# A blockwise causal attention feeding a gated FFN: zeros as weights of the warming matmuls, and three more head pairs transposed by DMA

## The chip, the cores and the metric

The kernel runs on one core of a Trainium2 chip. The metric is the device time of one execution in microseconds (us); lower is better. A core has a tensor engine (PE, with a separate row PEld for its weight loads), a vector engine (DVE), a scalar engine (ACT), a general engine (POOL) and a sync engine (SP) that here only issues DMAs. In the profile a name with a "q" (SPq, ACTq, POOLq) is the engine's instruction sequencer, which among other things issues DMAs; "L707" is line 707 of the kernel.

## The reference

Eight batches, eight heads, 576 tokens, head size 64. Attention is causal by blocks of 64 tokens; its output, with the heads side by side, is the input of a feed-forward layer with a ReLU gate.

```python
scores = scale * q @ k^T                      # per batch and head, 576 x 576
scores = where(block_i >= block_j, scores, -1e9)
attn = softmax(scores)
x = (attn @ v)  ->  [8 * 576, 512]            # tokens x (8 heads x 64)
out = (relu(x @ w_gate) * (x @ w_val)) @ w_out   # 512 -> 1536 -> 512
```

## The kernel before

The schedule is written out by hand: every engine executes its instructions in the order in which the program names them. The unit of the attention is a round `r` = 4 x batch + head pair, 32 rounds in all. Rounds 0 to 7 are written out one by one; rounds 8 to 31 are the loop at line 1008. Between the pieces of a round stand pieces of the FFN: `ffn(n)` takes the next matmuls from a generator that walks through the batches one after the other, so that PE always has work.

One round of the loop does, in this order on each engine:

1. `head_av(r - 1, 0)` (L648, PE): attention times values of the previous round's first head, with the exponentials in `attnT` as weights.
2. `scores_all(r)` (L514, PE): three pieces of scores into three pairs of PSUM banks, and four exponentials by ACT (L520) into one of two buffers `attnT`.
3. `head_av(r - 1, 1)`, then `heads_to_xnat(r - 1)`: a reciprocal and a product on DVE (L592, L593) write the normalised output, tokens on partitions, into the tile `xnat`. There are three `xnat` buffers, so round r + 3 writes the buffer of round r.
4. A transpose that puts features on partitions, as the FFN needs them: 512 tokens go into `xT` (three buffers, one per batch), the last 64 tokens of the batch into `xTt`. There are two ways. `to_xT_pe` takes one PSUM bank, five PE transposes (L693 four times, L699 once, with the identity matrix `ident`), and two ACT copies (L700, L702). `to_xT_dma` issues two DMA transposes on SP's queue (L707 and L711) that read `xnat` and write `xT` and `xTt`. `to_xT_dma` stands right behind step 3, `to_xT_pe` behind the first block of FFN matmuls.
5. In some rounds `unpermute` (two DVE copies, L407) for a later batch's q and k, which were transposed by DMA (L396, L438, L439) on SP's queue as well. They are issued for batch 3 at the end of round 8, ahead of anything that SP issues in rounds 9 to 12.
6. `corners(r)` (L579, L580, DVE): zeros in the masked corners of `attnT`. The next round's `head_av` waits for it.
7. FFN matmuls (L752: gate and value, L782: output projection), a ReLU on ACT (L761), a product on DVE (L766), and for each finished output a DVE copy into `ob` (L794, four buffers) and a store that ACT issues (L720). A store is issued one output later than its copy.

In batch 2 (rounds 8 to 11) all four head pairs go through `to_xT_pe`, in rounds 9 to 12; from batch 3 on all go through `to_xT_dma`. The FFN of batch 2 begins on PE in round 13, behind that round's scores. At the end of round 11 POOL issues the loads of batch 4 (`load_qkv`, L459 and L452), which convert fp32 to bf16 on the way and run in POOL's own DMA queue.

Three rules of the framework decide what waits for what. A PSUM bank, an `xnat`, `xT` or `ob` buffer is written again only when its last readers are done, and a DMA that reads it is a reader until it has landed. `take` hands out the six PSUM banks outside `head_av` by least recent use, so that leaving out a `take(1)` shifts which bank a later matmul gets. And every DMA that SP or ACT issues gets one of eight completion semaphores in turn, in the order of the program; it is issued only when the DMA that had that semaphore before it has landed. The sequencer of the engine stands still for that wait, and so does everything behind it in that engine's order.

At the start, `junk` (L831) runs matmuls of 512 columns of zeros into a bank that nothing reads, until the first q and k are there. Its weights are `ident`, which POOL makes with two instructions (`make_identity`); the moving operand is `zeros`, which DVE clears first of all (L108). Seven of them stand ahead of the first transposes of q and k (L423), two behind.

Of the kernel before, what the change touches and what calls it, by code (L numbers as in the profile page):

```python
# [17 lines left out]
def kernel(  # L18
# [29 lines left out]
    banks = psum.tile([128, 8, 512], FP, name="banks")  # L48
# [25 lines left out]
    ident = consts.tile([128, 128], BF)  # L74
# [32 lines left out]
    zeros = consts.tile([128, 128], BF, name="zeros")  # L107
# [7 lines left out]
    def constants(i, eng):  # L115
        eng.memset(v_bf[i][:, 0:4, :, 64:65], 1.0)
# [11 lines left out]
    def selection(zero, copy):  # L128

        zero(sel, 0.0)  # L130
        for c in range(4):
            ps = slice(32 * c, 32 * c + 32)

            copy(
                sel[ps, c % 2]
                .rearrange("p (j m) -> p j m", j=4)[:, :, 0:128]
                .rearrange("p j (h r) -> p j h r", h=2)[:, :, :, 0:16],
                ident[ps, None, 32 * c : 32 * c + 32]
                .to_broadcast([32, 4, 32])
                .rearrange("p j (h n) -> p j h n", h=2),  # L140
            )
# [388 lines left out]
    def scores_all(r, tails=True):  # L530

        b, hp = divmod(r, 4)
        at = attnT[r % 2]
        sc = scores(b, hp, pair(), [(0, 0, True)])
        for hh in range(2):
            exp(at[:, hh, 0:512], sc[:, hh, :])
        sc = scores(b, hp, pair(), [(0, 1, True), (384, 3, True)])
        exp(at[:, :, 512:1024], sc)
        sc = scores(
            b, hp, pair(),  # L540
            [(0, 2, True)]
            + [(256 + 64 * c, c, False) for c in range(4 if tails else 0)],
        )
        w = 512 if tails else 256
        exp(at[:, :, 1024 : 1024 + w], sc[:, :, 0:w])

    def scores_last(b):

        sc = take(1)[:, 0, 0:256]
        for hp in range(4):  # L550
            nc.tensor.matmul(
                sc[:, 64 * hp : 64 * hp + 64],
                kTt[b % 2][:, hp, :],
                qTt[b % 2][:, hp, :],
                start=True,
                stop=True,
            )
        exp(attnD[b % 2][:, 0:256], sc)
# [16 lines left out]
    def corners(r, eng):  # L575

        at = attnT[r % 2]
        three = at[64:128, :, 0:1536].rearrange("p g (c n) -> p g c n", c=3)
        eng.memset(three[:, :, :, 0:64], 0.0)  # L579
        eng.memset(at[64:128, :, 896:960], 0.0)  # L580
# [19 lines left out]
    def tails_av(b, hh):  # L600

        av = banks[:, AV + hh, 0:260].rearrange("p (n d) -> p n d", d=65)
        for hp in range(4):
            for c in range(NCH):
                col = 1024 * hh + 256 * hp + 64 * c
                w = (
                    attnE[:, col : min(col + 128, 2048)]
                    if c < 4
                    else attnD[b % 2][:, 64 * hp : 64 * hp + 128]
                )  # L610
                nc.tensor.matmul(  # L611
                    av[0 : w.shape[1], hp, :],
                    w,
                    v_bf[b % 2][:, c, 2 * hp + hh, :],
                    start=(hp == 0 and c == 0),
                    stop=(c == 4),
                    skip_group_check=True,
                )

    def tails_of(b, x):  # L620
        x = x[64 * b : 64 * b + 64]
        av = banks[0:64, AV : AV + 2, 0:260].rearrange("p g (n d) -> p g n d", d=65)
        normalise(x.rearrange("p n (h d) -> p h n d", h=2), av)
# [10 lines left out]
    def head_av(r, hh, bank=None):  # L634
        b, hp = divmod(r, 4)
        blocks = NCH if b > 1 else 4
        h = 2 * hp + hh
        vb = v_bf[b % 2]
        bank = banks[:, AV + hh : AV + hh + 1] if bank is None else bank
        av = bank[:, :, 0:325].rearrange("p g (n d) -> p g n d", d=65)  # L640
        for p in range(blocks):
            for c in range(p + 1):
                if p == 4 and c == 4:
                    w = attnD[b % 2][:, 64 * hp : 64 * hp + 128]
                else:
                    col = BASE[c] + 128 * (p - c) if p < 4 else TAIL + 64 * c
                    w = attn(r, col, col + 128)[:, hh, :]
                nc.tensor.matmul(  # L648
                    av[:, 0, p, :],
                    w,  # L650
                    vb[:, c, h, :],
                    start=(p == 0),
                    stop=(c == p),
                    skip_group_check=True,
                )
        return av[:, :, 0:blocks]
# [11 lines left out]
    def heads_to_xnat(r, bank=AV):  # L668

        blocks = NCH if r >= 8 else 4  # L670
        av = banks[:, bank : bank + 2, 0 : 65 * blocks].rearrange(
            "p g (n d) -> p g n d", d=65
        )
        normalise(
            xnat_of(r)[:, 0:blocks].rearrange("p n (h d) -> p h n d", h=2), av
        )
# [27 lines left out]
    def to_xT_dma(r):  # L704
        b, hp = divmod(r, 4)
        xnat = xnats[r]
        nc.sync.dma_start_transpose(  # L707
            xT_of(b)[:, hp, :].rearrange("p (c n) -> p c n", c=4),
            xnat[:, 0:4, :].rearrange("p c n -> p (c n)"),
        )  # L710
        nc.sync.dma_start_transpose(xTt[:, hp, b : b + 1, :], xnat[0:64, 4, :])  # L711
# [97 lines left out]
    def ffn(n):  # L809

        done[0] += n
        while part[0] < done[0]:
            ended = False
            while not ended:
                ended = next(gen, None)
                if ended is None:
                    return
                part[0] += 4
# [10 lines left out]
    def junk(n, bank):  # L829
        for _ in range(n):  # L830
            nc.tensor.matmul(  # L831
                bank.rearrange("p (j n) -> p j n", j=4),
                ident,
                zeros[:, None, :].to_broadcast([128, 4, 128]),
                start=True,
                stop=True,
            )
# [4 lines left out]
    with tc.manual_schedule(engines={E.PE, E.DVE, E.Activation, E.Pool, E.SP}):  # L842
# [10 lines left out]
        constants(0, nc.vector)  # L853
        constants_tail(0, nc.vector)
        selection(nc.vector.memset, nc.vector.tensor_copy)
        junk(7, banks[:, 0])
        constants(1, nc.gpsimd)
        constants_tail(1, nc.gpsimd)
        token_order(pool)
# [148 lines left out]
        for r in range(8, 4 * B):  # L1008
            b, hp = divmod(r, 4)
            tails_av(1, 0) if r == 8 else head_av(r - 1, 0)  # L1010
            scores_all(r)
            tails_av(1, 1) if r == 8 else head_av(r - 1, 1)
            tails_of(1, xt) if r == 8 else heads_to_xnat(r - 1)
            if r > 12:
                to_xT_dma(r - 1)
            if r < 10:
                e2.unpermute(r - 6, (dve, dve))
            elif 11 <= r < 15:
                e3.unpermute(r - 11, (dve, dve))
            corners(r, nc.vector)  # L1020
            ffn(12 if r < 13 else 8)
            if hp == 0:
                scores_last(b)
            if 8 < r < 13:
                to_xT_pe(r - 1, (act,))
            if r == 8:
                tails_to_xT(xt, dve)
                e2.cast_v_tail(pool)
                e2.cast_v_chunks(0, pool)
                e2.cast_v_chunks(1, pool)  # L1030
                e3 = Early(3)
                e3.load_qk(0, 4)
                e3.load_tails((0, 1))
                e3.load_qk(4, 4)
                e3.load_tails((2,))
                e3.load_v_chunks(0)
                e3.load_v_chunks(1)
                e3.cast_qk(0, 4, (pool, pool))
                e3.cast_tails((pool, pool))
                e3.cast_qk(4, 4, (pool, pool))  # L1040
                e3.transpose(0)
                e3.transpose(1)
                e3.transpose_tails()
            if r == 11:
                for g in range(2):
                    e3.cast_v_chunks(g, pool)
                e3.cast_v_tail(pool)
            if hp == 3 and b + 2 < B:
                load_qkv(b + 2, (0, 1))
            if b >= 3 and b + 1 < B:  # L1050
                if hp == 0:
                    load_qkv(b + 1, (2,))
                if hp == 2:
                    dma_transposes(b + 1)
            ffn(8 if r < 12 else 0 if r == 12 else 28)
# [32 lines left out]
```

## Time and profile before

| | |
|---|---|
| device time, three runs | 368.2, 368.8, 370.13 us (median 368.8) |
| the profiled execution | 367.89 us, of which its span is 366.1 us |
| PE busy | 355.9 us, 97% of the span |
| DVE, ACT, POOL busy | 167.6, 167.3, 114.8 us |
| HBM read, written | 37.75 MB, 9.44 MB |
| transposes of `xnat` on PE (L693 and L699) | 52 |
| DMA transposes of `xnat` (L707 and L711) | 20 and 20 |

The span is the time from the first to the last instruction of the core; the rest of an execution's time lies around it. Times in the trace are counted from the start of the span. A row of the timeline shows start, duration, engine, line, operation, output and input, and in brackets the idle time before it with what ended it. A row of the chain of waits shows start, duration and the instruction group that held up the end at that time. Matmuls are pipelined: the duration of one contains its way through the array, while the next begins long before; the chain counts only the time by which each pushes the next. For a DMA "us to landing" is counted from the start of its issue.

### The profile page before, as it was taken

To read this page: it belongs to the slowest core of one execution; us is meant where nothing else is said; L and a number is where in the kernel's file an instruction comes from. 1 tells how busy PE (TensorE), PEld (TensorE's weight loads), DVE (VectorE), ACT (ScalarE), POOL (GpSimd) and SP (SyncE) were. 2 spreads that over 40 slices of the span, in tenths; PEclk is the share of its full clock that TensorE was granted. 3 is DMA by queue.
4 is the path that set the end of the run, shared out by engine and by line. 5 is a ranking of instruction groups with operands and counts; after the bars stand their busy time and mean duration, and the time that the engine had idled before them with its cause. 6 is when DMAs were issued, how large, how long until landed. Compare 5 with 4: busy or idle time off the path is not lost.

```text
span 366.1 us, 7493 instructions
## 1 busy us (share of the span) xinstructions
PE 355.9 (97%) x2981; PEld 187.3 (51%) x2981; DVE 167.6 (46%) x335; ACT 167.3 (46%) x263; POOL 114.8 (31%) x158
## 2 busy tenths in 40 slices
PE   7899998999999999999999999999999999999995
PEld 3544455555555455555555555555555544444443
DVE  5744455466465543444344443544344424333432
ACT  4933716556756653565346543654264303302310
POOL 7756746275878307700590031000000000000000
PEclk9999999999999999999999999999999999999999
DMA  8999999979999979996899949173200130020013
GB/s 253 288 348 351 379 255 323 158 198 238 194 190 139 141 154 98 165 104 118 104 182 73 148 86 124 28 138 75 75 16 18 47 102 1 3 86 29 2 39 104
DMA packets 139652, 51.02 MB, mean 139 GB/s; under 512 B 117473, under 2 KB 133601, under 8 KB 139617
## 3 DMA queue, kind: packets, MB, share of 16 engines
q1 hardware_dynamic: 77952, 34.29, 41.1%
q0 software_dynamic: 56384, 7.08, 40.7%
q10 hardware_dynamic: 5280, 9.18, 7.1%
q8 instruction: 23, 0.38, 0.4%
q14 instruction: 13, 0.10, 0.1%
HBM read 37.75 MB, written 9.44 MB: 129 GB/s over the span
## 4 chain that ended last, share of the span: by engine, by line
PE 93%; ACT 4%; DVE 1%; issue 0%; POOL 0%; ACTq 0%; DVEq 0%; POOLq 0%
PE banks L752 51%; PE banks L782 25%; PE banks L648 7%; PE banks L514 6%; ACT attnT L520 2%; PE banks L831 1%; PE banks L611 1%; PE banks L693 1%; PE banks L423 1%; ACT wo L520 1%; ACT v_p L520 1%; PE banks L373 1%; DVE kTt L240 0%; DVE ob L794 0%; ACT xT L700 0%
## 5 line engine op out<-in xcount | busy, mean ns | idle before, releaser
L520 ACT ACTIVATE attnT<-banks 128x1024 bf16<-128x1024 f32 (+1 forms) x118 | 84.9, 808 | 59.7 <-PE banks L514 59.4
L761 ACT ACTIVATE gate_sb<-banks 128x512 bf16<-128x512 f32 x108 | 64.9, 603 | 102.4 <-PE banks L752 102.2
L766 DVE TENSOR_TENSOR hT<-gate_sb,banks 128x512 bf16<-128x512 bf16 x108 | 74.1, 687 | 80.5 <-PE banks L752 74.2
L752 PE MATMUL banks<-xT,wg 128*128 128x512 bf16 x384 | 99.6, 379 | 0.6 <-ACT attnT L520 0.4
L752 PE MATMUL banks<-xT,wv 128*128 128x512 bf16 x384 | 99.4, 379 | 0.0
L782 PE MATMUL banks<-wo,hT 128*128 128x512 bf16 (+1 forms) x444 | 97.2, 373 | 0.0
L752 PEld LDWEIGHTS <-wv 128*128 128x128 bf16 x432 | 42.1, 98 | 50.4 <-POOL wv L502 0.3
L782 PEld LDWEIGHTS <-hT 128*128 128x128 bf16 x444 | 42.3, 98 | 46.3 <-issue 0.2
L752 PEld LDWEIGHTS <-wg 128*128 128x128 bf16 x432 | 40.8, 98 | 46.3 <-issue 1.3
L794 DVE COPY ob<-banks 128x512 f32<-128x512 f32 (+1 forms) x37 | 25.1, 677 | 52.4 <-PE banks L782 52.3
L459 POOL DMA_DIRECT2D v_bf<-in_v_dram x16 | 14.3, 908 | 66.9 <-PE banks L648 66.9
L648 PE MATMUL banks<-v_bf,attnT 128*128 128x65 bf16 x792 | 33.4, 194 | 0.6 <-DVE attnT L579 0.3
L648 PEld LDWEIGHTS <-attnT 128*128 128x128 bf16 x792 | 29.1, 98 | 8.6 <-issue 1.0
L514 PE MATMUL banks<-qTm,kTm 64*128 64x512 bf16 (+3 forms) x256 | 25.0, 300 | 2.4 <-ACT attnT L520 1.5
L593 DVE TENSOR_TENSOR xnat<-banks,recip 128x640 bf16<-128x640 f32 (+2 forms) x36 | 25.9, 721 | 1.2
L514 PEld LDWEIGHTS <-kTm 64*128 64x128 bf16 x512 | 17.1, 94 | 10.8 <-issue 1.7
L592 DVE RECIPROCAL recip<-banks 128x10 f32<-128x10 f32 (+3 forms) x38 | 8.0, 210 | 31.2 <-PE banks L648 29.3
L459 POOL DMA_DIRECT2D k_bf<-in_k_dram x16 | 14.2, 928 | 1.7 <-DMA v_bf<-in_v_dram 1.1
L459 POOL DMA_DIRECT2D q_bf<-in_q_dram x16 | 14.4, 935 | 0.5 <-DMA v_bf<-in_v_dram 0.5
L579 DVE MEMSET attnT<- 64x192 uint32 x27 | 5.9, 218 | 18.0 <-ACT attnT L520 17.3
L752 PE MATMUL banks<-xTt,wg 128*128 128x512 bf16 x48 | 12.3, 379 | 0.0
L752 PE MATMUL banks<-xTt,wv 128*128 128x512 bf16 x48 | 12.3, 379 | 0.0
(99 smaller groups left out, 199.9 us busy)
## 6 DMA issues: line engine op xcount, KB each, us to landing
out_dram<-ob ACTq DMA_DIRECT2D x32, 256.0 KB, 2.4
stage<-in_moe_w_gate_dram SPq DMA_DIRECT2D x6, 512.0 KB, 8.7
stage<-in_moe_w_val_dram SPq DMA_DIRECT2D x6, 512.0 KB, 8.8
stage<-in_q_dram SPq DMA_DIRECT2D x6, 512.0 KB, 8.1
stage<-in_k_dram SPq DMA_DIRECT2D x6, 512.0 KB, 8.2
stage<-in_moe_w_out_dram SPq DMA_DIRECT2D x6, 512.0 KB, 9.5
stage<-in_v_dram SPq DMA_DIRECT2D x8, 256.0 KB, 6.7
q_bf<-in_q_dram POOLq DMA_DIRECT2D x16, 128.0 KB, 6.7
```

The source lines that it names most:

```text
L459: nc.gpsimd.dma_start(dst, src[b, :, 128 * c : 128 * c + n, :].rearrange("h p d -> p h d"),)
L514: nc.tensor.matmul(o, kTm[b % 2][ps, c, hp, :], x, start=True, stop=True)
L520: nc.scalar.activation(out, sc, AF.Exp, scale=scale)
L579: eng.memset(three[:, :, :, 0:64], 0.0)
L592: nc.vector.reciprocal(recip, av[:, :, :, 64])
L593: nc.vector.tensor_tensor(out=out, in0=av[:, :, :, 0:64], in1=recip.to_broadcast([rows, heads, n, 64]), op=AX.mult,)
L648: nc.tensor.matmul(av[:, 0, p, :], w, vb[:, c, h, :], start=(p == 0), stop=(c == p), skip_group_check=True,)
L752: nc.tensor.matmul(out[f][:, t, :], (wg, wv)[t][i][:, c, fo : fo + 128], x[:, c, :], start=(c == 0), stop=(c == 3),)
L761: nc.scalar.activation(gate[f], out[f][:, 0, :], AF.Relu)
L766: nc.vector.tensor_tensor(out=h, in0=gate[f], in1=out[f][:, 1, :], op=AX.mult)
L782: nc.tensor.matmul(ops[:, g, 0 : n1 - n0], hT[f][:, 128 * s : 128 * (s + 1)], wo[i][:, f % 4, n0:n1], start=(f == 0), stop=(f == 11),)
L794: nc.vector.tensor_copy(ob, ops[:, g, 0 : n1 - n0])
```

## The change

The warming matmuls use `zeros` as weights in place of `ident`, and there are nine ahead of the first transposes in place of seven (the later call with two stays). In rounds 9, 10 and 11 `to_xT_dma` takes the place of `to_xT_pe`; round 12 (batch 2's last head pair) stays with `to_xT_pe`, and rounds from 13 on are as before.

```diff
@@ junk
             nc.tensor.matmul(
                 bank.rearrange("p (j n) -> p j n", j=4),
-                ident,
+                zeros,
                 zeros[:, None, :].to_broadcast([128, 4, 128]),
@@ start
-        junk(7, banks[:, 0])
+        junk(9, banks[:, 0])
@@ rounds 8 to 31
-            if r > 12:
+            if r > 8 and r != 12:
                 to_xT_dma(r - 1)
...
-            if 8 < r < 13:
+            if r == 12:
                 to_xT_pe(r - 1, (act,))
```

As built, the program has 15 transposes less on PE and six copies less on ACT; DVE and POOL have the same instructions in the same order; SP has six DMA transposes more, which stand behind batch 3's L439 and ahead of round 13's L707. The completion semaphores are dealt out anew from there on. Three waits in the built program differ for that reason or for the buffers: the product L593 that writes round 11's output waits until round 8's two DMA transposes have landed (same `xnat` buffer), and likewise for the two rounds after it; the sixth store (L720), which stands in ACT's order ahead of round 12's exponentials, has the semaphore of round 8's L707 and waits for its landing (before: for a transpose of batch 3's q, L396); the seventh store, behind those exponentials, waits for round 8's L711.

## The prediction

> **What bounds the kernel now.** I read the page first: shares of the engines, and the shares of the chain that ended last.
>
> ```profile
> span 366.1 us, 7493 instructions
> PE 355.9 (97%) x2981; PEld 187.3 (51%) x2981; DVE 167.6 (46%) x335; ACT 167.3 (46%) x263; POOL 114.8 (31%) x158
> PE 93%; ACT 4%; DVE 1%; issue 0%; POOL 0%; ACTq 0%; DVEq 0%; POOLq 0%
> ```
>
> PE is the bound nearly everywhere. Next, what PE waited for; these are the two largest entries.
>
> ```profile
> PE banks L831 <- POOL ident masks.py:199: 2.0, 1, 2.0
> PE banks L514 <- ACT attnT L520: 1.5, 4, 0.6
> ```
>
> After the first 20 us almost nothing stops PE, so a matmul taken off it there shortens the run by the time it takes, and a new stop of PE lengthens it fully: no later idle time swallows it. The change touches two places, the start and rounds 9 to 13. The chain of waits shows the second place.
>
> ```profile
> 96.98 0.22 PE banks L693 x4
> 97.20 0.06 PE banks L699
> 97.25 0.45 PE banks L648 x15
> ...
> 106.29 2.59 PE banks L782 x12
> 108.88 0.12 PE banks L551 x4
> 108.99 0.22 PE banks L693 x4
> 109.22 0.06 PE banks L699
> 109.27 0.46 PE banks L648 x15
> ...
> 111.06 1.08 PE banks L752 x5
> ```
>
> Row follows row without a gap; 106.29 to 109.27 is the middle of round 12, 111.06 the first FFN matmul of batch 2.
>
> **The part removed from PE.** One set of transposes holds PE for 0.22 + 0.06 = 0.28 us. Three sets go: 0.84 us less, if nothing new waits. The six ACT copies that go as well ran beside PE and are worth nothing by themselves. The bank rotation shifts; the pieces of scores that wait for an `ob` copy or a product (L794, L766) keep their order, and the three pairs still rotate, so I take 0 for it, at most 0.1 us for each set that no longer separates a copy from the piece that waits for its bank.
>
> **The part added to SP's queue.** Where do the six DMA transposes fall, and when do they land? First the issues on SP's queue and, beside them, POOL's loads for batch 4, from the timeline.
>
> ```profile
> 98.84 1.27 SPq L439 DMA_TRANSPOSE kTt<-k_bt  x1
> 112.25 1.19 SPq L707 DMA_TRANSPOSE xT<-xnat  x1
> 113.49 1.22 SPq L711 DMA_TRANSPOSE xTt<-xnat  x1
> 99.68 3.56 POOL L459 DMA_DIRECT2D k_bf<-in_k_dram  x4
> ```
>
> SP's batch 3 transposes end with L439, issued until 98.84 + 1.27 = 100.11. Round 8's `xnat` is long written by then, but L707 must stand behind L439. So round 8's pair is issued at 100.2 and, at the pitch of the rows 112.25 and 113.49 (1.24 us), 101.4; round 9's at 102.7 and 103.9, round 10's at 105.2 and 106.4. In the kernel before, SP has nothing to issue from 100.2 to 112.25.
>
> Now the landings. The rows below are DMA issues in small windows (us from issue to landing at the end of the row), in the order of issue: L396 at 92.30, L439 at 98.84, POOL's loads at 100 to 101 and at 102 to 103, L707 at 112.25, L711 at 113.49; the last is the spread of all twenty L711.
>
> ```profile
> perm<-k_bf SPq DMA_TRANSPOSE x1, 4.2
> kTt<-k_bt SPq DMA_TRANSPOSE x1, 7.4
> k_bf<-in_k_dram POOLq DMA_DIRECT2D x2, 128.0 KB, 7.6
> k_bf<-in_k_dram POOLq DMA_DIRECT2D x2, 128.0 KB, 8.8
> xT<-xnat SPq DMA_TRANSPOSE x1, 7.6
> xTt<-xnat SPq DMA_TRANSPOSE x1, 7.5
> DMA to landing us min/median/max: 2.3/2.5/7.5
> ```
>
> A transpose usually lands after 2.5 us, but not here: while POOL's loads run it takes 7.4 to 7.6, as the loads themselves do. I take 7.6, because the neighbours in time on both sides and the loads of that very microsecond agree on it. Lower bound 4.2 (just before POOL's loads began), upper bound 8.8 (POOL's slowest). So round 8's L707 lands at 100.2 + 7.6 = 107.8, its L711 at 101.4 + 7.6 = 109.0.
>
> **Who waits for it.** Two engines, both in round 12. On DVE:
>
> ```profile
> 106.59 0.82 DVE L593 TENSOR_TENSOR xnat<-banks,recip 128x640 bf16<-128x640 f32 x1
> ...
> 108.97 0.11 DVE L580 MEMSET attnT<- 64x64 uint32 x1
> ```
>
> This L593 writes round 11's output into the `xnat` buffer of round 8, which both DMA transposes still read. It started at 106.59; now it cannot before 109.0. Behind it on DVE stand two L407 copies and the corner zeros; from its start to the end of L580 it is 108.97 + 0.11 - 106.59 = 2.49 us. So the corners are ready at 109.0 + 2.5 = 111.5, and `head_av(12, 0)`, which ran at 109.27 and waits for the corners, starts at 111.5 instead of 109.27 - 0.84 = 108.4. On ACT:
>
> ```profile
> 102.94 0.34 ACTq L720 DMA_DIRECT2D out_dram<-ob  x1
> 105.36 0.60 ACT L520 ACTIVATE attnT<-banks 128x512 bf16<-128x512 f32 x1 [2.72 <-PE banks L514]
> ```
>
> The store at 102.94 is the sixth. Now it waits for round 8's L707 (its completion semaphore), and ACT's sequencer stands with it until 107.8; round 12's first exponential, behind it in the order, moves from 105.36 to 107.8 and ends at 108.4. The L782 group at 106.29 (105.45 without the three sets) writes the bank that this exponential reads, so it starts at 108.4, ends at 111.0, and with 0.12 + 0.28 for L551 and the last PE set PE reaches `head_av(12, 0)` at 111.4. Two independent chains thus give 111.4 and 111.5; the later decides: 111.5 - 109.27 = +2.2 us, and 0.05 us for the semaphore makes it **+2.3 us**, the 0.84 us already in it.
>
> By the lower bound (4.2) L707 lands at 104.4 and L711 at 105.6: corners at 108.1, first exponential done at 105.0, both earlier than PE needs them, so -0.84. By the upper (8.8), L711 lands at 110.2, corners at 112.7: +3.4. The store that waits for L711 comes behind the exponentials and costs nothing. Nor does the next use: batch 2's FFN starts at 111.06 + 2.3 = 113.4 and needs round 10's `xT` (landing 105.2 + 7.6 = 112.8) two matmuls later; round 9's pair, down at 111.5, is out of the way of the `xnat` product at about 113.6.
>
> **The start.**
>
> ```profile
> 0.83 0.11 DVE L108 MEMSET zeros<- 128x64 uint32 x1 [0.83 <-PEq L1072]
> 1.97 3.17 PE L831 MATMUL banks<-zeros,ident 128*128 128x512 bf16 x7 [1.97 <-POOL ident masks.py:199]
> 4.41 0.43 DVE L326 CAST q_bf<-stage 128x512 bf16<-128x512 f32 x1
> ...
> 5.14 0.85 PE banks L423 x8
> 6.85 0.54 PE banks L514 x2
> 7.41 4.85 ACT attnT L520 x6
> ...
> 35.17 0.45 PE banks L423 x8
> ```
>
> `zeros` is ready at 0.94, so the warming begins near 1.0 instead of 1.97. Seven matmuls took 3.17 us, the last of them some 0.6 by itself, so one pushes the next by 0.43; nine push 3.85 and let go at 4.85, just when q is cast (4.41 + 0.43 = 4.84). The first transposes therefore start where they did, within 0.1 us. What can move is the clock: eight L423 took 0.85 us here and 0.45 later, so the clock was still low, and the first scores (0.54) could at most be halved. If it rises before the first transposes, 0.40 + 0.27 = 0.67 us is gained; if not before 7.41, nothing. Were zeros as weights to warm less, the small matmuls behind 7.41 would run low for longer, mostly beside ACT's exponentials (4.85 us for six): a loss of 0.3 at most, half of the 0.54. I take 0 in the sum: the new stop hangs on landings, and SP's queue up to 100.1 is not paced by the start of PE as far as I can see; where it is, up to 0.67 goes off.
>
> The Trainium skill (TensorE: Matmul & The Clock Gate, Part 1) says the clock rises after a busy window of about 3.4 us that runs free of the kernel's start. The trace fits: from 1.97 until behind 6.85 is more than one such window. By that rule an earlier start of 1 us gives, as an estimate, anything from nothing to the full 0.67 us, depending on the phase.
>
> **Sum.** 0 (start) - 0.84 (three sets) + 3.1 (the stop in round 12) = +2.3 us. The profiled execution's 367.89 would become 370.2. It lies 0.9 under the median of the runs (368.8), so for a median I say 368.8 + 2.3 = **371.1 us**.
>
> **Rivals.**
> - *Transposes in time.* The landings are as in the rows at 92.30 or quicker, and round 12 doesn't stop: it decides at a latency under about 4.6 us (L707 at 104.8). Then 368.8 - 0.84 = 368.0, or 367.4 with most of the start's gain. For it: the median of 2.5. Against: five rows of 7.4 and more around that moment.
> - *A backlog.* From 92.30 to 98.84 the latency rose by 3.2 us over four transposes, 0.8 for each. If that is a queue that grows, L711 of round 8 takes 9.0 (lands 110.4, +3.7), and round 10's L707 takes 11.4, landing at 116.6, while PE wants it at about 115.2: +5.1, 373.9 us. Against: L707 at 112.25, with nothing queued by SP for 13 us, is as slow, so it is the load of POOL's queue.
> - *The clock falls.* PE would stand still from 105.45 to 108.4, longer than anywhere in the trace (2.0). If the clock drops to the rate of the start, the L782 group takes 5.2 instead of 2.6 us: +4.9, 373.7 us. Against: no row of this trace shows the clock falling.
>
> This last rival is also what the Trainium skill (TensorE: Matmul & The Clock Gate, Why this matters for your kernels) warns of: no idle gap above about 3 us between bursts of matmuls. The gap forecast here is at that limit; no run here shows one.
>
> **How the numbers follow.** Forecast 0.65 (landings of 6.5 to 8.8: 369.9 to 372.2), in time 0.13, backlog 0.12, clock 0.10. The range holds the forecast, the start's bounds and most of each rival: 367.9 to 373.5. About 0.5% (1.84 us) is what a measurement here can tell from no change. Slower by more: two thirds of the forecast (0.43) and both upward rivals make 0.64; within: the rest of the forecast and half of "in time", 0.30; faster by more needs that rival and the start's gain together: 0.06.
>
> **What would show it.** In the profile after: L831 starting near 1.0; L707 at about 100.2 and landing after about 7.6 us; L593 at 109 with a DMA transpose of `xnat` as what it waited for; ACT idle until 107.8 ahead of round 12's first exponential; PE idle before the L782 group of about 3 us and a little ahead of L648. It is wrong if those transposes land within 4.6 us, or if PE's idle time in round 12 is small although they land late.

## The result, and the profile after

| | before | after |
|---|---|---|
| device time, median (range) | 368.98 us (368.2 to 370.13), 6 runs | 374.75 us (372.36 to 379.47), 6 runs |
| ratio after / before, 95% interval | | 1.0141 [1.0098, 1.0184] |
| span of the first profiled execution | 366.1 us | 370.6 us |

The change makes the kernel slower by 1.4%, some 5.8 us between the medians. The forecast was 371.1 us with a range up to 373.5: the sign was right, the loss 2.5 times the forecast. The slowest of the six runs after, 379.47 us, counts as a slow one and is left out of the ratio.

The page of the first profiled execution after (span, busy time, granted clock in 40 slices of 9.3 us):

```profile
span 370.6 us, 7474 instructions
PE 358.6 (97%) x2968; PEld 187.1 (50%) x2968; DVE 168.2 (45%) x335; ACT 165.5 (45%) x257; POOL 114.8 (31%) x158
PEclk9999996999999999999999999999999999999999
```

PE has 15 transposes fewer and two warming matmuls more, and is busy 2.7 us longer: where the time went is partly not in waits but in the clock, which has a 6 in one slice near 60 us. Before, that row has only nines:

```profile
PEclk9999999999999999999999999999999999999999
```

The granted clock after by stretches (start to end in us; length; busy time and count of PE, PEld, DVE, ACT, POOL; clock; DMA share; GB/s):

```profile
58.00:60.00 2.00, 1.33 (x15) 0.87 (x14) 1.43 (x5) 2.00 (x5) 0.03 (x1) 0.66 1.08 390
60.00:64.00 4.00, 4.00 (x20) 1.72 (x16) 1.29 (x2) 1.01 (x2) 2.75 (x6) 0.50 1.17 327
64.00:66.00 2.00, 2.00 (x9) 0.74 (x8) 0.00 (x0) 0.00 (x0) 2.00 (x3) 0.63 1.01 216
```

The clock stood at half for 1.36 + 4 + 1.48 = 6.8 us. PE reaches round 9, whose first L648 is at 84.97 us in the timeline of before, at 89.21. The same group in the chains of waits, before and after:

```profile
85.13 0.45 PE banks L648 x15
```

```profile
89.37 0.46 PE banks L648 x15
```

Of these 4.2 us, 1.2 were lost before the clock fell: in the same chains the first L240 behind 55 us is at 56.22 before and at 57.45 after. The fall accounts for the other 3.0. And the stop that was forecast for round 12 is almost absent here, as the chain of waits shows:

```profile
98.40 1.96 PE banks L782 x10
100.36 8.53 DMA xT<-xnat
...
109.41 0.60 ACT attnT L520
...
110.06 2.75 PE banks L782 x12
```

Everything of the forecast mechanism is in these rows: L707 issued at 100.36, landed at 108.89, the store behind it, the exponential at 109.41, the L782 group at 110.06. But PE, already late by 4.2 us, has only 0.3 us to wait. One profile would thus suggest that the loss is a fall of the clock near 58 us and that the transposes cost nothing. Three more profiles of the same kernel, the last experiment below, show the stop in round 12, and that this execution is the odd one of the four.

### The profile page after: what moved, and what is told of

Read it like the earlier page. It is cut to its first block, busy times and chain, and to the rows that moved or that the text cites. A ratio compares the mean times of both kernels' runs of the same rounds, so it can differ in the third digit from the quotient of the medians.

```text
span 370.6 us, 7474 instructions
## 1 busy us (share of the span) xinstructions
PE 358.6 (97%) x2968; PEld 187.1 (50%) x2968; DVE 168.2 (45%) x335; ACT 165.5 (45%) x257; POOL 114.8 (31%) x158
## 4 chain that ended last, share of the span: by engine, by line
PE 87%; DMA 7%; DVE 2%; ACT 1%; SPq 1%; POOL 1%; issue 0%; ACTq 0%; DVEq 0%; POOLq 0%
PE banks L752 49%; PE banks L782 24%; PE banks L648 6%; PE banks L514 5%; DMA stage<-in_moe_w_val_dram 2%; DMA xT<-xnat 2%; DMA stage<-in_v_dram 1%; ACT attnT L520 1%; DMA stage<-in_k_dram 1%; PE banks L611 1%; SPq L279 1%; PE banks L373 1%; DVE ob L794 0%; DVE kTt L240 0%; PE banks L693 0%
## 5 line engine op out<-in xcount | busy, mean ns | idle before, releaser
L766 DVE TENSOR_TENSOR hT<-gate_sb,banks 128x512 bf16<-128x512 bf16 x108 | 74.0, 687 | 81.3 <-PE banks L752 74.6
L752 PE MATMUL banks<-xT,wg 128*128 128x512 bf16 x384 | 99.4, 379 | 1.2 <-POOL wg L502 0.7
L752 PE MATMUL banks<-xT,wv 128*128 128x512 bf16 x384 | 99.4, 379 | 0.1
L782 PE MATMUL banks<-wo,hT 128*128 128x512 bf16 (+1 forms) x444 | 99.1, 379 | 0.3 <-ACT attnT L520 0.3
L752 PEld LDWEIGHTS <-wv 128*128 128x128 bf16 x432 | 42.1, 98 | 50.7 <-POOL wv L502 0.6
L782 PEld LDWEIGHTS <-hT 128*128 128x128 bf16 x444 | 43.0, 99 | 48.6 <-issue 3.6
L752 PEld LDWEIGHTS <-wg 128*128 128x128 bf16 x432 | 40.8, 98 | 46.8 <-POOL wg L502 0.9
L648 PE MATMUL banks<-v_bf,attnT 128*128 128x65 bf16 x792 | 33.4, 194 | 1.2 <-POOL v_bf L340 0.6
L648 PEld LDWEIGHTS <-attnT 128*128 128x128 bf16 x792 | 29.2, 98 | 9.5 <-issue 1.1
L514 PE MATMUL banks<-qTm,kTm 64*128 64x512 bf16 (+3 forms) x256 | 25.4, 299 | 2.0 <-DVE kTm L435 0.6
L593 DVE TENSOR_TENSOR xnat<-banks,recip 128x640 bf16<-128x640 f32 (+2 forms) x36 | 26.0, 721 | 1.2
L514 PEld LDWEIGHTS <-kTm 64*128 64x128 bf16 x512 | 16.8, 94 | 10.4 <-issue 1.5
L752 PE MATMUL banks<-xTt,wg 128*128 128x512 bf16 x48 | 12.3, 379 | 0.0
L752 PE MATMUL banks<-xTt,wv 128*128 128x512 bf16 x48 | 12.3, 379 | 0.0
```

The lines of the kernel that those rows point to most:

```text
L514: nc.tensor.matmul(o, kTm[b % 2][ps, c, hp, :], x, start=True, stop=True)
L593: nc.vector.tensor_tensor(out=out, in0=av[:, :, :, 0:64], in1=recip.to_broadcast([rows, heads, n, 64]), op=AX.mult,)
L648: nc.tensor.matmul(av[:, 0, p, :], w, vb[:, c, h, :], start=(p == 0), stop=(c == p), skip_group_check=True,)
L752: nc.tensor.matmul(out[f][:, t, :], (wg, wv)[t][i][:, c, fo : fo + 128], x[:, c, :], start=(c == 0), stop=(c == 3),)
L766: nc.vector.tensor_tensor(out=h, in0=gate[f], in1=out[f][:, 1, :], op=AX.mult)
L782: nc.tensor.matmul(ops[:, g, 0 : n1 - n0], hT[f][:, 128 * s : 128 * (s + 1)], wo[i][:, f % 4, n0:n1], start=(f == 0), stop=(f == 11),)
```

## The experiments

In kernels to which lines were added the numbers shift: with the fourth buffer (alone or together with the moved stores) L707, L711, L752 and L782 become L711, L715, L756 and L786; with held loads L514, L648, L707, L752 and L782 become L516, L651, L710, L755 and L785.

### One part at a time

The start alone (the change without its second half):

> Only the start is changed (nine warming matmuls of zeros alone); all transposes of batch 2 stay on PE. Theory A (a stop of PE in round 12, from late DMA transposes): this kernel has none of them, so it takes 368.3 to 369.0 us, ratio 0.998 to 1.001, clock 0.998 or more. Theory B (the earlier start makes PE run dry near 55 us for so long that its clock falls to half until about 65 us): 372 to 374 us, clock 0.986 to 0.992, L782 behind L373 near 61 us at twice its time, and PE about 4 us late in round 9.

The DMA transposes alone (the change without its first half):

> Only the transposes of batch 2's first three head pairs go to DMA; the start is as before. Theory A: round 8's L707 is issued at about 100.2 and lands 7.5 to 8.5 us later, the first exponential of round 12 starts at 108 to 109.4, the L782 group behind it at 108.6 to 110.1 instead of 106.29: +2.3 to +3.8 us, 371.1 to 372.8 us, clock 0.998. Theory B: without the changed start nothing stops, the three sets are saved: 368.0 to 368.3 us.

| | median (range), runs | ratio, 95% interval |
|---|---|---|
| start alone | 367.72 us (367.41 to 369.18), 10 | 0.9978 [0.9958, 0.9999] |
| transposes alone | 374.91 us (373.67 to 376.5), 4 | 1.0171 [1.0127, 1.0215] |

The start alone costs nothing (368.3 to 369.0 us were expected), and the transposes carry the whole loss. They cost more than theory A expected (371.1 to 372.8 us), which had no fall of the clock in it. Their chain of waits shows the place without the early fall of the clock:

```profile
101.07 7.79 DMA xT<-xnat
...
109.38 0.61 ACT attnT L520
...
110.03 0.43 PE banks L782
110.46 0.22 issue
110.68 3.79 PE banks L782 x10
114.46 0.12 PE banks L551 x4
```

In the timeline of PE the L782 at 110.03 carries 3.40 us of idle time, ended by ACT's exponential:

```profile
105.76 0.29 PE L514 MATMUL banks<-qTt,kTm 64*128 64x64 bf16 x8 [0.61 <-DMA qTt<-q_bt]
...
110.03 0.43 PE L782 MATMUL banks<-wo,hT 128*128 128x512 bf16 x1 [3.40 <-ACT attnT L520]
```

And the stretches show that the clock falls behind this stop:

```profile
104.00:108.00 4.00, 2.01 (x47) 1.45 (x45) 0.91 (x2) 0.00 (x0) 1.53 (x3) 1.00 1.85 149
108.00:112.00 4.00, 1.75 (x5) 0.74 (x6) 1.83 (x3) 2.62 (x4) 3.16 (x4) 0.78 1.73 185
112.00:116.00 4.00, 4.00 (x48) 2.27 (x46) 0.98 (x3) 1.55 (x5) 1.49 (x3) 0.80 1.64 219
```

Stretches that lie wholly inside a fall show 0.50, as 60 to 64 us of the first profile did; so 0.78 and 0.80 over 4 us each mean half a clock for 1.76 + 1.6 = 3.4 us. From 110.03 to 114.46 the L782 group takes 4.43 us; before it took 2.59. So the loss in round 12 has two parts of its own: 3.40 us of standing still and 1.84 us of running slowly afterwards.

### Which of the two waits decides

VectorE's wait alone removed: round 11's product goes to a tile that is free by then.

```diff
+        if r == 11:
+            xnats[r] = sel.rearrange("p a b -> p (a b)")[:, 0:640]...
```

> The DMA transposes alone, and round 11's product goes to a fourth buffer (the tile `sel`, which nothing reads any more by then), so that VectorE's L593 no longer waits for round 8's L711. Theory A (the store's wait in front of round 12's exponentials decides; the fall of the clock comes from the stop): no change beside the DMA transposes alone, 373.7 to 376.0 us; L593 of round 11 starts near 106.9 us instead of 109.56, but the L782 group of round 12 still starts near 110.0. Rival C (VectorE's wait for the buffer decides): the stop goes, 368 to 370 us.

ScalarE's wait alone removed: batch 1's stores on SyncE.

```diff
-            (STORE if j == 0 else nc.scalar).dma_start(out[r0 : r0 + 128, :], ob)
+            (STORE if j != 1 else nc.sync).dma_start(out[r0 : r0 + 128, :], ob)
```

> The DMA transposes alone, with batch 1's stores issued by SyncE instead of ScalarE, so that no exponential stands behind a store that waits; VectorE's wait for the buffer is left in. Theory A: the exponentials of round 12 start near 106.5 us instead of 109.38 and the L782 group near 107; VectorE's wait for L711 then stops PE a little later, ahead of round 12's first product, which starts near 112.6 us instead of 114.86 (109.27 before the change). 371.5 us if the clock holds, 373.3 us if it falls again. Rival C: no change, 373.7 to 376.0 us.

Both edits together:

> The DMA transposes alone, with both waits taken away: round 11's product in a fourth buffer and batch 1's stores issued by SyncE. Theory A: no stop in round 12, its L782 group starts near 106.5 us and its first product near 109.3, no fall of the clock there, 367.8 to 369.3 us, as before the change. Rival D (the DMA transposes cost by their traffic or on their own queue, whoever waits for them): 371 us or more.

| | median (range), runs | ratio, 95% interval |
|---|---|---|
| fourth buffer | 374.45 us (373.95 to 375.62), 4 | 1.0162 [1.0128, 1.0196] |
| stores on SyncE | 373.29 us (371.95 to 375.29), 4 | 1.0142 [1.0088, 1.0197] |
| both | 372.00 us (370.84 to 374.78), 8 | 1.0102 [1.0071, 1.0132] |

Timeline of PE with the fourth buffer, then VectorE's in the same execution:

```profile
109.93 5.28 PE L786 MATMUL banks<-wo,hT 128*128 128x512 bf16 x12 [4.31 <-ACT attnT L520]
```

```profile
105.92 0.82 DVE L593 TENSOR_TENSOR sel<-banks,recip 128x640 bf16<-128x640 f32 x1
```

VectorE no longer waits, and PE resumes at 109.93 as before that edit: ScalarE's chain is the one that decides, and VectorE's is hidden behind it. With the stores moved, PE's timeline:

```profile
110.71 0.40 PE L693 MATMUL banks<-ident,xnat 128*128 128x128 bf16 x4 [2.10 <-DVE xnat L593]
...
112.04 0.60 PE L648 MATMUL banks<-v_bf,attnT 128*128 128x65 bf16 x14 [0.87 <-DVE attnT L579]
...
115.09 0.59 PE L752 MATMUL banks<-xT,wg 128*128 128x512 bf16 x2 [0.65 <-DMA xT<-xnat]
```

The exponentials start on time, at 104.99, and VectorE's chain takes over as expected: L593 at 109.83, round 12's first product at 112.04 instead of 109.11. The stop is in two pieces of 2.10 and 0.87 us, and the clock stays at 1.00 in this execution (372.12 us); two of the other three runs took 374.46 and 375.29 us with mean granted clocks of 0.989 and 0.991. A third wait appears at 115.09: batch 2's first FFN matmuls want round 10's `xT`.

With both removed, the expectation of 367.8 to 369.3 us failed, and theory A with it in its simple form. The profile is of the slowest of the eight runs, 374.78 us:

```profile
107.32 0.29 PE L514 MATMUL banks<-qTt,kTm 64*128 64x64 bf16 x8 [2.36 <-DMA qTt<-q_bt]
...
116.41 0.72 PE L756 MATMUL banks<-xT,wg 128*128 128x512 bf16 x2 [3.02 <-DMA xT<-xnat]
```

The earlier PE is, the more it waits for the next late landing: round 10's L707, issued at 107.82, landed near 116.4. And batch 3's tail transpose L438, which the change doesn't touch, landed 9.3 us after its issue in this execution (6.0 in the profile of before). So the waits are symptoms; what they share is that nothing on SP's queue lands in time. That left the question of what makes the landings slow.

### What makes the landings slow

Batch 4's loads by POOL wait until round 11's product is written:

```diff
+                if (b, t, c) == (4, 0, 0):
+                    after(ins, product[0])     # ins: the load; product[0]: the last L593
...
-            if hp == 3 and b + 2 < B:
+            if hp == 3 and b + 2 < B and r != 11:
                 load_qkv(b + 2, (0, 1))
+            if r == 12:
+                load_qkv(4, (0, 1))
```

> The DMA transposes alone, and POOL's loads of batch 4's q and k, which start at 95.4 us before the change and run beside these transposes, wait until round 11's product is written (near 106 us). Theory F (the landings are late because these loads' packets stand before those of the transposes on the same DMA engines): the tails' L438 and round 8's L707 land within 3 to 4 us of their issue, by some 104 us, neither ScalarE nor VectorE nor PE stops in round 12, the first product of round 12 starts near 109 us, 367.8 to 369.5 us. Rival D (the queue of SyncE itself is slow, whatever POOL loads): L707 still lands after 7 us or more, 372 us or more.

Landings of the first three DMA transposes of `xT` (L707, issued from 101.1 to 106.6) with the transposes alone:

```profile
DMA to landing us min/median/max: 7.7/7.8/7.8
```

and with POOL's loads held back (L710, issued from 99.3 to 104.7), followed by PE's timeline:

```profile
DMA to landing us min/median/max: 2.7/2.9/3.6
```

```profile
107.92 0.59 PE L651 MATMUL banks<-v_bf,attnT 128*128 128x65 bf16 x14
...
139.50 0.72 PE L516 MATMUL banks<-qTm,kTm 64*128 64x512 bf16 x8 [1.90 <-DMA kTm<-k_bf]
140.60 0.29 PE L516 MATMUL banks<-qTt,kTm 64*128 64x64 bf16 x8 [0.39 <-DMA qTt<-q_bt]
```

The mechanism of the late landings is settled by this: the same transposes on the same queue, 7.8 us beside POOL's loads and 2.9 us without them (2.6 to 4.6 us in the two kernels below that hold the loads back as well). There is no stop in rounds 9 to 13, and round 12's first product starts at 107.92, ahead of the 109.11 of before. The Trainium skill (DMA: Bandwidth & Descriptors, Queues, rings and completion order) says that each DMA engine takes turns between the queues it has work for, packet by packet; the trace agrees insofar as the landing depends on what POOL's queue holds.

The time was not what I expected (373.55 us, 369.72 to 375.66, ratio 1.0154 [1.0094, 1.0214]; 367.8 to 369.5 expected). The profile is of the fastest of the four runs, 369.72 us; the others, up to 375.66 us, were not traced, and what they lost beyond it is open. In the profile the loads, and batch 5's behind them, run beside batch 4's own transposes, and the stop has moved to round 16: 1.90 + 0.39 us at 139.5. The whole change with the same loads held shows the same, and lost the second expectation too:

> The whole change, with POOL's loads of batch 4's q and k held back as in the run above. Theory F with the start's gain: 367.0 to 368.7 us, faster than the kernel before by a third of a per cent or so. Rival B (the changed start brings the clock down near 58 us): 370 us or more with a granted clock of 0.99 or less.

It took 371.59 us (370.87 to 373.65, 5 runs), ratio 1.0091 [1.0058, 1.0124], with a stop of 2.40 us at round 16. Its profile, of the slowest of the five runs (373.65 us), also has the sign that rival B named: a fall of the clock near 58 us, with round 9's first L648 at 86.47 us; a second fall lies behind the stop. Holding back every batch's loads until the first round of the batch before it answers the stop:

```diff
+                if (t, c) == (0, 0):
+                    after(ins, product[0])
...
-            if hp == 3 and b + 2 < B:
-                load_qkv(b + 2, (0, 1))
...
-                    load_qkv(b + 1, (2,))
+                    load_qkv(b + 1, (0, 1, 2))
```

> The whole change, with POOL's loads of every batch from the fifth on held until the product ahead of that batch's first weight products is written (rounds 12, 16, 20, 24), so that neither the transposes of rounds 9 to 11 nor the next batch's L468 run beside loads. Theory F: no stop of PE in rounds 9 to 16, the three sets are ahead by 0.84 us and the start by some 0.5 us: 366.5 to 368.0 us, ratio 0.995 to 0.998. Rival G (the loads are only moved, and some later transposes of a batch meet them): a stop of 2 us or so at a later round's L514, with a fall of the clock behind it, 370 us or more.

Measured: 367.98 us (366.84 to 371.57, 12 runs) beside 368.09 us, ratio 1.0004 [0.9979, 1.0029]. From round 9 to the end no stop of 0.2 us ended by a DMA is left, and the 1.4% are regained, but a gain over the kernel before cannot be told (a ratio of 0.995 to 0.998 was expected). The profiled execution, 369.05 us, begins round 9 only at 86.51 us instead of 84.97, behind a fall of the clock near 58 us:

```profile
58.00:60.00 2.00, 2.00 (x18) 1.32 (x18) 0.30 (x3) 1.73 (x3) 0.21 (x1) 0.50 1.07 372
60.00:64.00 4.00, 3.78 (x36) 2.09 (x36) 1.76 (x3) 0.00 (x0) 3.82 (x7) 0.84 1.03 263
```

From there to the end of the span it needs 280.8 us, the kernel before 281.1. Why so little is left of three sets of transposes, which give 0.89 us from round 8's first product to round 12's, is seen in a wait that every kernel with the DMA transposes has in round 14; here in the chain of waits of the transposes alone:

```profile
124.04 0.70 DVE hT L766
...
124.78 0.38 PE banks L514 x8
```

With fewer calls of `take` a piece of that round's scores gets a bank that VectorE's product L766 has just begun to read. From the round's first L648 to its second head's it takes 1.70 us in the timeline (123.39 to 125.09) where before it took 1.33 (117.81 to 119.14); the paced kernel has the same 1.70 (118.46 to 120.16). In the transposes alone round 10 shows a second such wait, 1.71 instead of 1.33 us, in the paced kernel 1.48.

### The price of the fallen clock

The stop was to be filled with matmuls of `ident` into unread columns of a bank, 56 of them, first ahead of round 12's weight products, then ahead of round 11's second product:

```diff
+            if r == 12:
+                warm(56)        # nc.tensor.matmul(banks[:, 7, 384:512], ident, ident)
             tails_av(1, 1) if r == 8 else head_av(r - 1, 1)
```

> The DMA transposes alone, and 56 matmuls of the identity into columns that nobody reads, placed on PE ahead of round 12's weight products, where it stops for 3.4 us. Theory A: the stop stays (the L782 group of round 12 starts near 110.0 us), but PE is not idle in it and the granted clock stays at 1.00 from 108 to 116 us; the group runs in 2.6 us instead of 3.8, and the time falls by some 1.6 us beside the DMA transposes alone, to 372.0 to 373.5 us. Rival E (the fall of the clock isn't from the stop): the clock still falls and the time stays at 373.7 us or more.

> As the kernel with 56 warming matmuls, but these stand ahead of round 11's second product on PE, where nothing holds them. Theory A: they fill the stop from 106 to 109 us, the exponentials and L711 still end near 109.5, the L782 group of round 12 starts near 110 us at a clock that stays up and takes 2.6 us instead of 3.8; the first product of round 12 starts near 113.2 us instead of 114.86; 372.0 to 373.5 us. Rival E (the fall isn't from the stop): granted clock under 0.9 in 108 to 116 us as before, 373.7 us or more.

The first try missed: 378.06 us (376.91 to 380.88, 4 runs), ratio 1.0267 [1.0215, 1.0318]. The warming matmuls write the bank that L593 was still to read, so they themselves waited, 3.69 us, and then ran at the fallen clock. They say nothing on the question. The second (373.04 us, 372.02 to 374.17, 4 runs, ratio 1.0122 [1.0085, 1.0159]) does:

```profile
104.53 3.30 PE L842 MATMUL banks<-ident 128*128 128x128 bf16 x56
...
109.80 2.75 PE L782 MATMUL banks<-wo,hT 128*128 128x512 bf16 x12 [1.50 <-ACT attnT L520]
```

PE still waits for ScalarE until 109.80, but idles only 1.50 us, and the granted clock is 1.00 in each stretch from 104 to 116. The group takes 2.58 us, from 109.80 to 112.38, instead of 4.43. Useless matmuls in the gap are worth 1.85 us there: the clock's share of the loss. The medians differ by as much, 1.9 us, but the intervals of the two ratios overlap, so the run times alone would not show it.

### The start

> Only the weights of the warming matmuls are changed to zeros, seven of them as before. If the start's gain comes from PE's beginning near 1.0 us instead of 1.97: the first exponential starts at 6.4 to 6.9 us instead of 7.41, as with nine (6.50), and the time is that of the changed start, 367.4 to 368.2 us. If it comes from the number: 7.2 to 7.5 us, and the time of before.

> Nine warming matmuls, still with the identity as weights. If the start's gain comes from PE's beginning earlier: the first exponential starts at 7.2 to 8.0 us, no earlier than before, 368.0 to 369.3 us. If from the number: 6.4 to 6.9 us, and 367.4 to 368.2 us.

Timelines of PE and ACT, with zeros as weights and seven matmuls, and then with the identity and nine:

```profile
1.00 3.17 PE L831 MATMUL banks<-zeros 128*128 128x512 bf16 x7 [1.00 <-DVE zeros L108]
...
6.50 3.44 ACT L520 ACTIVATE attnT<-banks 128x1024 bf16<-128x1024 f32 x4 [0.30 <-PE banks L514]
```

```profile
1.97 3.69 PE L831 MATMUL banks<-zeros,ident 128*128 128x512 bf16 x9 [1.97 <-POOL ident masks.py:199]
...
7.10 2.43 ACT L520 ACTIVATE attnT<-banks 128x1024 bf16<-128x1024 f32 x3 [0.30 <-PE banks L514]
```

With zeros as weights and seven matmuls, the first exponential comes at 6.50 us as with nine (6.51); with the identity and nine it comes at 7.10, with seven 7.41 in the profile of before. That would say that beginning at 1.00 moves it and that the number adds little. But the first exponential wanders from execution to execution of the same start. In the kernel with the useless matmuls ahead of round 11's second product, whose start is that of before, it comes as early:

```profile
6.52 3.44 ACT L520 ACTIVATE attnT<-banks 128x1024 bf16<-128x1024 f32 x4 [0.30 <-PE banks L514]
```

In the eight profiles with the unchanged start it lies between 6.52 and 7.43 us, six of them from 7.28 on; in the seven with zeros and nine between 6.50 and 7.14, five of them up to 6.62. The changed start usually brings it earlier, then, but one profile each cannot say whether the weights or the number do it. At the end nothing of it is certain: 368.13 us (ratio 1.0010 [0.9989, 1.0031]) and 369.03 us (1.0015 [0.9985, 1.0044]). Where it goes in the start alone is seen at the first idle place that both kernels have later, in PE's timeline before and with the start alone:

```profile
55.05 0.87 PE L232 MATMUL banks<-ident,perm 128*128 128x128 bf16 x8 [0.42 <-POOL perm L213]
```

```profile
55.11 0.87 PE L232 MATMUL banks<-ident,perm 128*128 128x128 bf16 x8 [0.77 <-ACT attnT L520]
```

PE comes earlier, idles longer, and goes on at the same time. Two things were left unfollowed: why the profile with seven matmuls of zeros is still 0.46 us ahead at 84.51 us and yet has before's span, and the 0.2% of the start alone, whose interval ends at 0.9999.

### The changed kernel three times more

> The changed kernel itself, profiled again. Theory H (the fall of the clock near 58 us in its first profile came by chance, and the stop in round 12 is the change's own price): here PE reaches round 12 near 105 us, stands still for some 3.5 us before its L782 group, and the clock falls behind that stop, between 108 and 116 us; no fall near 58 us in two of the three repeats at least. Rival B (the changed start brings the fall near 58 us): it is there in all three, PE reaches round 12 near 109.5 us and stops for 0.3 us.

> As the first repeat: by H a stop of some 3.5 us in round 12 with the fall of the clock behind it; by B the fall near 58 us and a stop of 0.3 us.

> As the first repeat: by H a stop of some 3.5 us in round 12 with the fall of the clock behind it; by B the fall near 58 us and a stop of 0.3 us.

377.62, 374.13 and 377.62 us. None has the fall near 58 us; each has the stop in round 12, of 7.38, 3.93 and 6.63 us. Chain of waits of the first of them:

```profile
101.55 10.54 DMA xT<-xnat
...
113.25 4.84 PE banks L782 x12
```

of the second:

```profile
100.57 7.64 DMA xT<-xnat
...
109.37 5.22 PE banks L782 x12
```

and of the third:

```profile
102.17 10.01 DMA xT<-xnat
...
113.34 4.75 PE banks L782 x12
```

Theory H holds: the usual loss of the changed kernel is the stop and the half clock at it, not the start. Rival B is refuted as it stood, with the fall near 58 us in every execution. A weaker form is open: that fall is in three of the eight profiles with zeros as weights (the first of the changed kernel, its variant with held loads, the paced kernel) and in none of the nine with the identity, so the changed start may make it more likely. In the run times of the start alone no loss shows. What differs between executions is the landing of round 8's L707, 7.64 to 10.54 us after its issue, and how long the clock stays down.

## Why the prediction was wrong

The step that failed is the term for the stop in round 12, 3.1 us in the sum. With the transposes alone the two stops and the slow running behind them measured 0.61 + 3.40 + 1.84 = 5.85 us: L707 landed at 108.9 us instead of 107.8, and the half clock was left out.

- *The mechanism* was as forecast in each link: L707 behind L439 (issued at 100.2 by the forecast, 100.4 to 102.2 measured), landing late, the sixth store waiting for it on ScalarE, VectorE's L593 waiting for the buffer, PE stopped in round 12. Each chain was shown alone.
- *Which chain decides* was called the wrong way round, by 0.1 us, and that mattered little: ScalarE's decides; VectorE's, forecast to give 111.5 us for the first product, gave 112.04 when it stood alone.
- *The landing* is the first mis-sized term. It was taken as 7.6 us with an upper bound of 8.8. The four profiles of the changed kernel have 7.64, 8.53, 10.01 and 10.54, the transposes alone 7.79 (there most of the delay is a late issue, 101.07 instead of 100.2). The bound came from rows of a single execution.
- *The clock* is the second. The forecast put the fall of the clock as a rival at 0.10, because no row of the trace showed one. It is the usual outcome: three of the four profiles of the changed kernel have it at the stop. The execution with the landing as forecast, 7.64 us, took 374.13 us; that rival was worked out as 373.7. The rule of the Trainium skill (TensorE: Matmul & The Clock Gate, Why this matters for your kernels) was named there and given too little weight: a gap forecast at 3 us stood right at its limit. Here stops of 3.02 us and more went with half a clock, those of 1.50, 2.10 and 2.36 us did not; in the whole change with held loads 2.40 us and, 0.7 us later, another 0.50 were enough.
- *"Nor does the next use"* was wrong: round 10's `xT` was forecast to be down at 112.8, and PE to come after. With the stores moved it landed at 115.1, with both waits gone near 116.4, where it cost 3.02 us; otherwise it is covered only because PE is late.
- *The transposes taken off PE*, 0.84 us: a little more. From round 8's first product to round 12's, the kernel with held loads needs 107.92 - 84.83 = 23.09 us, the kernel before 109.11 - 84.97 = 24.14: 1.05 us less. But the bank rotation, put at 0 and at most 0.1 us for a set, takes back 0.37 us in round 14 and up to 0.38 in round 10.
- *The start*, 0 in the sum: right within what can be told. In the profile of the start alone the first exponential came 0.9 us earlier, more than the upper bound of 0.67, but it varies by as much with the unchanged start; by 55 us nothing of it was left.
- *A backlog* in SP's queue is refuted: with the transposes alone three L707 in a row landed after 7.7 to 7.8 us, and without POOL's loads after 2.7 to 3.6.

In the transposes alone, from before's 366.1 to 372.2 us of span: the two stops of 0.61 and 3.40 and the slow group's 1.84 make 5.85, the three sets give back 1.05, two bank waits take 0.75; that is 5.55 of the 6.1 us, and the rest is not traced to a place.

## What to carry to other kernels

An instruction that is moved from a full engine to a DMA queue must be costed with the latency that the queue has at that moment, and a latency read beside heavy loads has a tail: take the worst of several executions, not the spread within one. Forecast a stop of PE with what follows it: near 3 us the clock's fall belongs in the sum, not among the rivals. And when a late landing has several waiters, remove the cause (the loads beside it) instead of the waits, and look where those loads go. Profile more than one execution: here the first of the changed kernel hid the stop, and single profiles of the start said more than they could.

## What the runs showed of the hardware

- The clock stays down for multiples of 3.4 us. In the stretches of the first repeat it is half for 0.72 + 4 + 4 + 1.5 = 10.2 us, from inside a stop of 7.38 us on:

```profile
104.00:108.00 4.00, 1.59 (x34) 1.08 (x32) 0.58 (x2) 0.00 (x0) 2.37 (x4) 0.91 1.79 176
108.00:112.00 4.00, 0.00 (x0) 0.00 (x0) 0.00 (x0) 0.00 (x0) 1.51 (x2) 0.50 2.65 100
112.00:116.00 4.00, 2.75 (x7) 0.99 (x7) 2.17 (x5) 2.92 (x4) 2.38 (x3) 0.50 1.85 146
116.00:120.00 4.00, 4.00 (x58) 2.43 (x57) 0.69 (x1) 1.62 (x5) 3.22 (x4) 0.81 1.99 215
```

  The stops of 3.02, 3.40 and 3.69 us went with 3.4 us of it, those of 3.93, 4.31 and 6.63 with 6.8, and the fall in the first profile lasted 6.8. It costs only where PE works: at the stop of 7.38 us the L782 group took 4.84 us, at that of 3.93 it took 5.22.
- The clock can also fall without a stop of that length: from 54 to 58 us of the first profile PE was busy for 2.49 of 4 us, with idle pieces of 1.10 us at most; in the paced kernel, whose clock fell there too, for 2.40 with pieces of 0.57 at most. The three repeats, as idle in the same place (2.18 to 2.45 of 4), kept it.
- A DMA transpose that is issued beside another queue's loads takes 2.7 times as long as by itself (7.8 against 2.9 us), although each of the two L707 groups moves the same data.
- What makes the landing 7.64 us in one execution and 10.54 in another of the same kernel was not settled.
